# The order of two softmax steps in batches 0 and 1, and who copies the last sums

## The chip, the cores and the metric

The kernel runs on one core of a Trainium2 chip. The metric is the device time of one execution in microseconds (us); before the change it is 493.74 us, the median of three runs (493.57 to 494.34). Four engines matter here: TensorE (PE, with its weight loads as PEld), VectorE (DVE), ScalarE (ACT), and the queue of SyncE (SP), which issues most transfers.

## The reference

Two parts run one behind the other. The first is an attention between 512 tokens `x` and 32 states of each of 8 heads in 8 batches, in both directions; the second takes its result, as 4352 rows of 512 numbers, through a bilinear layer and two products.

```python
scores = scale * np.matmul(x, state.transpose(0, 1, 3, 2))
a = softmax(scores)          # over the 32 states
xread = np.matmul(a, state)
scores2 = scale * np.matmul(state, x.transpose(0, 1, 3, 2))
a2 = softmax(scores2)        # over the 512 tokens
sread = np.matmul(a2, x)
...
h = (x @ w1) * (x @ w2) @ w3
out = h @ w_out
```

(`softmax` stands for the three lines of the reference that subtract the maximum, take the exponential and divide by the sum plus 1e-9.)

## The kernel before, in words

**Precision.** Each large product is made of float32 values split in two, a high part that ACT casts (L98) and a low part that DVE takes as the difference (L99). PE then multiplies low by high, high by high and high by low.

**The stages.** At first w3 and w_out are multiplied together (L559 and L572), once for all batches, while DVE and ACT convert the float64 weights (L119 to L135) that arrive by transfers. Then come the batches. For each one, the states times w1 and w2 give `sw` (L148, split at L98 and L99), and the softmax over the states gives `at`. Their product is *stage 1* (L311): eight blocks of 128 hidden features, each with a w1 half and a w2 half in one PSUM tile `ps`. ACT copies the first half (L292), DVE multiplies it with the second (L293), and the product is split into `g_hi` and `g_lo`. *Stage 2* multiplies these with the combined weights (L325 in `project`) and stores the result. Batch 0 goes this plain way: behind each pair of blocks, `early_stage2` already does stage 2 of that pair for two of the four token tiles. Batches 1 to 7 do stage 2 in quarters (`quarter_batch`), with fewer products.

**The softmax of a batch** is a generator, `scores` in `attention_steps`, that is advanced in pieces between other work. PE makes one PSUM tile of scores (L148), in which a row is a state and a column a token. Both softmaxes start from it. For the one over the tokens, DVE takes the *token maxima* of each row (L188) and scales them (L189), and ACT takes the exponentials with them (L197) into `e`. For the one over the states, DVE *turns* the scores in 32 by 32 blocks into the tile `work` (L191), takes the maxima over the states there (L204), subtracts them (L205), and ACT takes the exponential (L208); sums, reciprocals and a multiplication follow (L213 to L216), and a second turn (L221) gives what is split into `at`. Last, DVE turns `e` into `blocks` (L228), and 16 transfers on SP (`move_blocks`, L172) lay the blocks of 32 out anew, for PE's `read_state` (L243).

**Buffers.** The tiles named `work` have two buffers. For batch 1, the turn of L191 writes into the buffer that batch 0's 16 transfers of `move_blocks` read, so it waits for all of them. The PSUM tiles of two banks have three buffers.

**What sets the order.** On PE and SP the instructions stand as the code issues them. On DVE and ACT a scheduler orders them by when it reckons that they can start and by priority, except in the opening, up to `order.close()` (L631), where they too stand as written; batch 0's softmax lies there up to the split of `at`. Batch 1's softmax is issued in `side_steps`: its first three pieces stand between blocks 4 and 5 of batch 0, right behind stage 2 of blocks 2 and 3. `PLAIN` is 1.

**The last sums.** `state_rows` handles the 256 rows of `sread` at the very end. Its two calls of `stage2` store to four places each, so `store` takes its second branch (L341 and L342): ACT copies the left half of the sums out of PSUM, DVE the right half, and then four transfers of 64 KB go out, two from ACT's queue and two from SP's (L344).

Of the kernel before, what the change touches and what calls it, by code (L numbers as in the profile page):

```python
# [27 lines left out]
ALU = mybir.AluOpType  # L28
AX = mybir.AxisListType
# [7 lines left out]
PLAIN = 1  # L37

@with_exitstack
def attn_bilinear_kernel(  # L40
# [10 lines left out]
    nc = tc.nc  # L51
# [5 lines left out]
    FT, DO = w34_k.shape[0], out.shape[2]  # L57
# [4 lines left out]
    SCALE = 1.0 / math.sqrt(D)  # L62
# [26 lines left out]
    def bank():  # L89
        return ps_o.tile([P, NF], F32, name="ps_o")  # L90

    def two_banks():
        return ps_2.tile([P, 2, NF], F32, name="ps_2")

    def split(hi, lo, src):

        return (
            nc.scalar.copy(out=hi, in_=src),  # L98
            nc.vector.tensor_tensor(out=lo, in0=src, in1=hi.bitcast(F32), op=ALU.subtract),  # L99
        )  # L100
# [41 lines left out]
    def per_head(ps, b, moving):  # L142


        for j in range(NP):
            for q in range(KT):
                rows = slice(q * D, (q + 1) * D)
                nc.tensor.matmul(  # L148
                    ps[j * NS:(j + 1) * NS, q], sts[b][rows, j], moving(rows, j), start=True, stop=True
                )  # L150
# [14 lines left out]
    def work_tile():  # L165
        return att.tile([P, KT, S], F32, name="work")
# [9 lines left out]
    def attention_steps(b):  # L176
        xd = x_tiles[b]
        a2 = {}

        def scores():  # L180

            ps = two_banks()
            per_head(ps, b, lambda rows, j: xd[rows, j])
            yield
            flat = lambda t: t.rearrange("p k s -> p (k s)")

            m2 = att.tile([P, KT], F32, name="m2")
            nc.vector.tensor_reduce(out=m2, in_=ps, axis=AX.X, op=ALU.max)  # L188
            nc.vector.tensor_scalar_mul(m2, m2, -SCALE)  # L189
            s1 = work_tile()  # L190
            nc.vector.transpose(out=flat(s1), in_=flat(ps))  # L191
            e2 = att.tile([P, KT, S], F32, name="e2", bufs=1)
            sum2 = att.tile([P, KT], F32, name="sum2")
            a2["e"], a2["sum"] = e2, sum2
            for kt in range(KT):
                one = slice(kt, kt + 1)
                nc.scalar.activation(  # L197
                    out=e2[:, kt], in_=ps[:, kt], func=AF.Exp, bias=m2[:, one], scale=SCALE, accum_out=sum2[:, one]
                )

            J = KT * S // NS
            s1v = flat(s1).rearrange("p (j n) -> p j n", n=NS)
            m1 = att.tile([P, J], F32, name="m1")
            nc.vector.tensor_reduce(out=m1, in_=s1v, axis=AX.X, op=ALU.max)  # L204
            nc.vector.tensor_tensor(  # L205
                out=s1v, in0=s1v, in1=m1.unsqueeze(2).broadcast_to([P, J, NS]), op=ALU.subtract
            )
            nc.scalar.activation(out=s1, in_=s1, func=AF.Exp, scale=SCALE)  # L208
            yield
            nc.vector.tensor_scalar_add(sum2, sum2, 1e-9)  # L210
            nc.vector.reciprocal(out=sum2, in_=sum2)
            sum1 = att.tile([P, J], F32, name="sum1")
            nc.vector.tensor_reduce(out=sum1, in_=s1v, axis=AX.X, op=ALU.add)  # L213
            nc.vector.tensor_scalar_add(sum1, sum1, 1e-9)
            nc.vector.reciprocal(out=sum1, in_=sum1)
            nc.vector.tensor_tensor(  # L216
                out=s1v, in0=s1v, in1=sum1.unsqueeze(2).broadcast_to([P, J, NS]), op=ALU.mult
            )
            yield
            at = work_tile()  # L220
            nc.vector.transpose(out=flat(at), in_=flat(s1))  # L221
            at_tiles[b] = [att.tile([P, KT, S], F32R, name=f"at_{part}", bufs=1) for part in ("hi", "lo")]
            last = split(*at_tiles[b], at)
            yield

            blocks = work_tile()
            with tc.issue_after(last[1].ins):
                nc.vector.transpose(out=flat(blocks), in_=flat(e2))  # L228
            a2["t"] = work_tile() if b < PLAIN else att.tile([P, KT, S], F32, name="e2", bufs=1)
            tiles = lambda t: t.rearrange("p k (t m) -> p (k t) m", m=P)  # L230
            move_blocks(lambda its, j: tiles(a2["t"])[its, :, j * NS:(j + 1) * NS],
                        lambda mine, c: tiles(blocks)[mine, :, c * NS:(c + 1) * NS])

        def read_state():

            xs = token_tiles[b]

            ps = (bank() if b else two_banks()[:, 0])[:, :KT * D].rearrange("p (k d) -> p k d", k=KT)
            for kt in range(KT):
                for t in range(NT):  # L240
                    for j in range(NP):
                        mine = slice(j * NS, (j + 1) * NS)
                        nc.tensor.matmul(  # L243
                            ps[mine, kt], a2["t"][:, kt, t * P + j * NS:t * P + (j + 1) * NS],
                            xs[:, t, 2 * j + kt], start=(t == 0), stop=(t == NT - 1),
                        )
            scaled = att.tile([P, KT, D], F32, name="scaled", bufs=1)
            a2["read"] = nc.vector.tensor_tensor(
                out=scaled, in0=ps, in1=a2["sum"].unsqueeze(2).broadcast_to([P, KT, D]), op=ALU.mult
            )  # L250
            turned = att.tile([P, KT, D], F32, name="turned")
            nc.vector.transpose(
                out=turned.rearrange("p k d -> p (k d)"), in_=scaled.rearrange("p k d -> p (k d)")
            )
            yield
            move_blocks(lambda its, j: sread[its, j, b * NS:(b + 1) * NS],
                        lambda mine, c: turned.rearrange("p k (c n) -> p (k c) n", n=NS)[mine, c])

        return scores, read_state, a2


# [25 lines left out]
    last_split, stored = [], []  # L287
# [47 lines left out]
    def store(ps, dests):  # L335
        o = main.tile([P, NF], F32, name="tmp", bufs=4)[:, :DO]
        with tc.high_priority():
            if len(dests) == 1:
                stored[:] = [nc.scalar.copy(out=o, in_=ps[:, :DO])]
            else:  # L340
                nc.scalar.copy(out=o[:, :DO // 2], in_=ps[:, :DO // 2])  # L341
                nc.vector.tensor_copy(out=o[:, DO // 2:], in_=ps[:, DO // 2:DO])  # L342
        for (dest, first, n), queue in zip(dests, cycle((nc.scalar, nc.sync))):
            queue.dma_start(out=dest, in_=o[first:first + n])  # L344

# [308 lines left out]
    for tt in range(NT):  # L654
        dests = [(out[0, tt * P:(tt + 1) * P], 0, P)]
# [85 lines left out]
```

## Time and profile before

| | |
|---|---|
| median of three runs | 493.74 us |
| the profiled execution, its own time | 493.72 us |
| its span, first to last instruction | 491.9 us |
| granted clock of TensorE in the span | 1.0 |
| turn (L191), 8 times | 1.23 us each |
| token maxima (L188), 8 times | 1.19 us each |

Rows of the timeline give the start in us from the span's start, the length, the engine, the line, the operation and its tiles (out<-in), their shape and how many instructions are merged; a bracket at the end is the idle time of the engine in front of it, and what ended that. Rows with SPq or ACTq are issues of transfers. A row of the chain of waits has start, length, engine, tile and line. Most of the lines stand for many instructions, so the start tells which one is meant.

### The profile page before, as it was taken

What the parts mean: (1) busy time and instruction counts of PE and PEld (TensorE: products, weight loads), DVE (VectorE), ACT (ScalarE), POOL (GpSimd) and SP (SyncE); (2) the same over time, 40 slices, a digit from 0 to 9 for tenths busy, and PEclk for the clock granted to TensorE, in tenths of its full rate; (3) what the DMA queues carried; (4) which work ended last, traced back from release to release, by engine and by line L of the source; (5) the groups of instructions that cost most, each with busy time, mean ns of one, the idle gap of its engine ahead of it and who ended that gap; (6) DMA issues with size and microseconds to landing.
All of it is one profiled execution on the core that took longest, in us unless ns stands there. A gap on an engine that the chain in (4) does not pass through costs nothing.

```text
span 491.9 us, 8604 instructions
## 1 busy us (share of the span) xinstructions
PE 483.7 (98%) x3390; PEld 368.3 (75%) x3390; DVE 391.4 (80%) x578; ACT 238.2 (48%) x364; POOL 0.2 (0%) x4
## 2 busy tenths in 40 slices
PE   7999999999999999999999999999999999999996
PEld 5444467667787878787878788877887788899885
DVE  5759897779799879957995899589859985578870
ACT  4867784443367144704570456055605550354640
POOL 0000000000000000000000000000000000000000
PEclk9999999999999999999999999999999999999999
DMA  8994971143104414130413042204220222001101
GB/s 342 414 418 135 373 294 28 16 186 86 42 7 177 105 29 179 19 102 15 179 37 94 5 180 49 81 5 179 50 79 6 89 54 75 7 2 43 45 2 43
DMA packets 56361, 52.49 MB, mean 107 GB/s; under 512 B 42752, under 2 KB 50944, under 8 KB 51712
## 3 DMA queue, kind: packets, MB, share of 16 engines
q1 hardware_dynamic: 47488, 43.27, 26.3%
q10 hardware_dynamic: 8832, 8.65, 5.1%
q8 instruction: 27, 0.44, 0.4%
q14 instruction: 14, 0.11, 0.1%
HBM read 38.27 MB, written 8.91 MB: 96 GB/s over the span
## 4 chain that ended last, share of the span: by engine, by line
PE 78%; DVE 7%; SPq 6%; ACT 5%; DMA 3%; issue 1%; ACTq 0%; DVEq 0%
PE ps L311 29%; PE ps_o L429 11%; PE ps L441 8%; SPq L172 6%; PE ps L148 6%; PE ps_o L434 5%; PE ps L446 4%; PE ps L679 3%; PE ps_o L559 3%; PE ps L559 3%; PE ps_o L325 2%; PE ps L681 2%; ACT ulps L127 2%; DMA raw<-in_w_dram 1%; ACT w_sb L119 1%; PE ps_o L243 1%
## 5 line engine op out<-in xcount | busy, mean ns | idle before, releaser
L311 PE MATMUL ps<-at_lo,sw_hi 128*128 128x512 f32 x256 | 101.8, 397 | 0.2 <-ACT e L197 0.2
L311 PE MATMUL ps<-at_hi,sw_hi 128*128 128x512 f32 x256 | 99.9, 390 | 0.0
L311 PE MATMUL ps<-at_hi,sw_lo 128*128 128x512 f32 x256 | 99.7, 389 | 0.0
L518 ACT COPY tmp<-ps 128x512 f32<-128x512 f32 x56 | 32.8, 585 | 126.0 <-PE ps L311 115.3
L311 PEld LDWEIGHTS ps<-at_lo,sw_hi 128*128 128x128 f32 x256 | 48.1, 188 | 17.6 <-DVE g_x L398 4.4
L311 PEld LDWEIGHTS ps<-at_hi,sw_lo 128*128 128x128 f32 x256 | 48.1, 188 | 10.3
L311 PEld LDWEIGHTS ps<-at_hi,sw_hi 128*128 128x128 f32 x256 | 48.1, 188 | 9.5 <-issue 0.2
L457 DVE TENSOR_TENSOR tmp<-tmp,ps 128x512 f32<-128x512 f32 x42 | 28.9, 688 | 17.3 <-PE ps L446 16.3
L398 DVE TENSOR_TENSOR g_x<-tmp,ps 128x512 f32<-128x512 f32 x28 | 19.1, 681 | 28.7 <-ACT tmp L518 28.7
L99 DVE TENSOR_TENSOR sw_lo<-ps,sw_hi 128x1024 fp32r<-128x1024 f32 (+1 forms) x34 | 38.2, 1145 | 0.2 <-ACT sw_hi L98 0.2
L98 ACT CAST g_hi<-raw 128x512 fp32r<-128x512 f32 x42 | 24.1, 618 | 23.2 <-DVE raw L398 14.3
L98 ACT CAST sw_hi<-ps 128x1024 fp32r<-128x1024 f32 (+1 forms) x34 | 31.1, 964 | 2.9 <-PE ps L148 2.7
L429 PEld LDWEIGHTS ps_o<-wo,g_hi 128*128 128x128 f32 x224 | 28.2, 191 | 5.6 <-issue 5.0
L99 DVE TENSOR_TENSOR g_lo<-raw,g_hi 128x512 fp32r<-128x512 f32 x42 | 28.0, 681 | 4.9 <-PE ps_o L434 2.8
L429 PEld LDWEIGHTS ps_o<-t,g_hi 128*128 128x128 f32 x224 | 27.8, 192 | 5.0 <-issue 5.0
L98 ACT CAST g_hi<-g_x 128x512 fp32r<-128x512 f32 x42 | 25.9, 620 | 11.5 <-DVE g_x L398 6.0
L148 PE MATMUL ps<-w_sb,st 64*32 64x512 f32 (+1 forms) x544 | 31.4, 570 | 0.0
L429 PE MATMUL ps_o<-t,g_hi 128*128 128x256 f32 x224 | 29.8, 286 | 0.0
L429 PE MATMUL ps_o<-wo,g_hi 128*128 128x256 f32 x224 | 29.7, 286 | 0.0
L99 DVE TENSOR_TENSOR g_lo<-g_x,g_hi 128x512 fp32r<-128x512 f32 x42 | 27.4, 679 | 1.8 <-PE ps_o L434 1.8
L572 PE MATMUL ps_o<-w_sb,w 128*128 128x512 f32 x64 | 28.5, 599 | 0.2 <-DVE w L135 0.2
L441 PE MATMUL ps<-t,g_hi 128*128 128x512 f32 x112 | 28.0, 392 | 0.0
(105 smaller groups left out, 784.4 us busy)
## 6 DMA issues: line engine op xcount, KB each, us to landing
raw<-in_w_k_dram SPq DMA_DIRECT2D x8, 1024.0 KB, 5.9
x_d<-in_x_d_dram SPq DMA_DIRECT2D x8, 1024.0 KB, 6.6
raw<-in_w_dram SPq DMA_DIRECT2D x8, 1024.0 KB, 6.4
x_s<-in_x_s_dram SPq DMA_DIRECT2D x8, 1024.0 KB, 5.0
out_dram<-tmp ACTq DMA_DIRECT2D x56, 128.0 KB, 1.8
raw<-in_w3t_dram SPq DMA_DIRECT2D x4, 1024.0 KB, 5.1
e<-work SPq DMA_DIRECT2D x112, 32.0 KB, 2.0
sread<-turned SPq DMA_DIRECT2D x128, 4.0 KB, 1.7
```

Of the source, the lines that this page charges most:

```text
L98: nc.scalar.copy(out=hi, in_=src),
L99: nc.vector.tensor_tensor(out=lo, in0=src, in1=hi.bitcast(F32), op=ALU.subtract),
L148: nc.tensor.matmul(ps[j * NS:(j + 1) * NS, q], sts[b][rows, j], moving(rows, j), start=True, stop=True)
L172: nc.sync.dma_start(out=dest(slice(c * NS, (c + 1) * NS), j), in_=src(slice(j * NS, (j + 1) * NS), c))
L311: nc.tensor.matmul(ps[:, i], w[:, kt, c:c + P], a[:, kt], start=(k == 0), stop=(k == 3 * KT - 1))
L429: nc.tensor.matmul(ps[:, tt * HO:(tt + 1) * HO], g, w(part, k), start=(fresh and k == 0 and tt == 0 and part == "lo"), stop=False, skip_gr ...
L434: nc.tensor.matmul(ps[:, tt * HO:(tt + 1) * HO], g, w("hi", k), start=False, stop=(k == QF - 1), skip_group_check=True)
L441: nc.tensor.matmul(ps[:, tt].rearrange("p (n d) -> p n d", n=2), g, w(k), start=(k == 0), stop=False, skip_group_check=True,)
L457: sum2 = lambda out, x, y: nc.vector.tensor_tensor(out=out, in0=x, in1=y, op=ALU.add)
L518: nc.scalar.copy(out=a_sb, in_=ps[:, 0])
L559: nc.tensor.matmul(w34_ps[i][:, :DO], chunks[k][:, DO + i * P:DO + (i + 1) * P], w_out[k], start=(k == 0), stop=(k == FT - 1),)
L572: nc.tensor.matmul(w34_ps[i][:, :DO], w3s[i][:, k * P:(k + 1) * P], w_out[k], start=(k == 0), stop=(k == FT - 1))
```

## The change

In `scores`, the buffer for the turned scores is taken ahead of the one for the maxima, and the two groups of steps, the turn on one side and the token maxima with their scaling on the other, become two small functions. Batches 0 and 1 call the turn first, batches 2 to 7 the maxima first, as all of them did before. In `store` the branch with two engines goes, and ACT copies the whole width of the sums in all cases.

```diff
+            s1 = work_tile()
             m2 = att.tile([P, KT], F32, name="m2")
-            nc.vector.tensor_reduce(out=m2, in_=ps, axis=AX.X, op=ALU.max)
-            nc.vector.tensor_scalar_mul(m2, m2, -SCALE)
-            s1 = work_tile()
-            nc.vector.transpose(out=flat(s1), in_=flat(ps))
+
+            def turn():
+                nc.vector.transpose(out=flat(s1), in_=flat(ps))
+
+            def maxima():
+                nc.vector.tensor_reduce(out=m2, in_=ps, axis=AX.X, op=ALU.max)
+                nc.vector.tensor_scalar_mul(m2, m2, -SCALE)
+
+            for step in (maxima, turn) if b > PLAIN else (turn, maxima):
+                step()
...
-            if len(dests) == 1:
-                stored[:] = [nc.scalar.copy(out=o, in_=ps[:, :DO])]
-            else:
-                nc.scalar.copy(out=o[:, :DO // 2], in_=ps[:, :DO // 2])
-                nc.vector.tensor_copy(out=o[:, DO // 2:], in_=ps[:, DO // 2:DO])
+            stored[:] = [nc.scalar.copy(out=o, in_=ps[:, :DO])]
```

The lines behind the first edit stand 7 lower in the changed kernel, those behind the second 3 lower: the exponentials of L197 are L204 there, L204 is L211, L205 is L212, L293 is L300, L213 is L220; the turn is L191 in both, the maxima are L194 and their scaling L195.

In the order of DVE, batch 0 has the five steps in the old order, and then in the new one (`ps_226` are the scores, `work` the turned scores, the `m` tiles the maxima):

```order
L188 TENSOR_REDUCE m_256<-ps_226 128x2
L189 TENSOR_SCALAR m_256<-m_256 128x2
L191 STREAM_TRANSPOSE work<-ps_226 128x1024
L204 TENSOR_REDUCE m_265<-work 128x32
L205 TENSOR_TENSOR work<-work,m_265 128x1024
```
```order
L191 STREAM_TRANSPOSE work<-ps_226 128x1024
L194 TENSOR_REDUCE m_257<-ps_226 128x2
L195 TENSOR_SCALAR m_257<-m_257 128x2
L211 TENSOR_REDUCE m_265<-work 128x32
L212 TENSOR_TENSOR work<-work,m_265 128x1024
```

What stands in front and behind is the same; the scaling now stands between the maxima and the maxima over the states.

In the order of DVE, batch 1, from the first step behind block 4 of batch 0 on. `ps_609` are batch 1's scores, `ps_638` and `ps_658` blocks 5 and 6 of batch 0 as PE leaves them; the `g_lo` in these rows is block 5's low part. Before, and then now:

```order
L188 TENSOR_REDUCE m_618<-ps_609 128x2
L191 STREAM_TRANSPOSE work<-ps_609 128x1024
L189 TENSOR_SCALAR m_618<-m_618 128x2
L204 TENSOR_REDUCE m_627<-work 128x32
L205 TENSOR_TENSOR work<-work,m_627 128x1024
L293 TENSOR_TENSOR tmp<-tmp,ps_638 128x512
L210 TENSOR_SCALAR sum_624<-sum_624 128x2
L211 RECIPROCAL sum_624<-sum_624 128x2
L213 TENSOR_REDUCE sum_633<-work 128x32
L293 TENSOR_TENSOR tmp<-tmp,ps_658 128x512
L99 TENSOR_TENSOR g_lo<-tmp,g_hi 128x512
L214 TENSOR_SCALAR sum_633<-sum_633 128x32
```
```order
L191 STREAM_TRANSPOSE work<-ps_609 128x1024
L194 TENSOR_REDUCE m_619<-ps_609 128x2
L211 TENSOR_REDUCE m_627<-work 128x32
L300 TENSOR_TENSOR tmp<-tmp,ps_638 128x512
L195 TENSOR_SCALAR m_619<-m_619 128x2
L212 TENSOR_TENSOR work<-work,m_627 128x1024
L99 TENSOR_TENSOR g_lo<-tmp,g_hi 128x512
L300 TENSOR_TENSOR tmp<-tmp,ps_658 128x512
L217 TENSOR_SCALAR sum_624<-sum_624 128x2
L218 RECIPROCAL sum_624<-sum_624 128x2
L220 TENSOR_REDUCE sum_633<-work 128x32
L99 TENSOR_TENSOR g_x<-tmp,g_x 128x512
```

Block 5's product moved from behind the subtraction to the place ahead of it, and its low part from behind the sums (L213) to right behind the subtraction; the turn with its wait for transfers moved ahead of the maxima.

In the order of ACT at the same place, from the cast of block 4's high part on (`ps_638` and `ps_658` as above; the first `g_hi` row is block 4's, the second block 5's). Before, and then now:

```order
L98 CAST g_hi<-tmp 128x512
L197 ACTIVATE e_623,sum_624<-ps_609,m_618 128x512
L292 COPY tmp<-ps_638 128x512
L197 ACTIVATE e_623,sum_624<-ps_609,m_618 128x512
L208 ACTIVATE work<-work 128x1024
L292 COPY tmp<-ps_658 128x512
L98 CAST g_hi<-tmp 128x512
```
```order
L98 CAST g_hi<-tmp 128x512
L299 COPY tmp<-ps_638 128x512
L98 CAST g_hi<-tmp 128x512
L204 ACTIVATE e_623,sum_624<-ps_609,m_619 128x512
L299 COPY tmp<-ps_658 128x512
L204 ACTIVATE e_623,sum_624<-ps_609,m_619 128x512
L215 ACTIVATE work<-work 128x1024
```

Block 5's copy and cast now stand ahead of the exponentials; before, the cast stood behind L208.

Besides, block 7 of batch 0 takes the PSUM buffer that block 5 had, where before it took that of batch 1's scores; the first read of a state takes that one now. PE's order and SP's are the same as before.

## The prediction

> **What bounds the kernel now.** The page's table of engines comes first, then the timeline of the tensor engine (PE), its rows with an idle time in brackets.
>
> ```profile
> PE 483.7 (98%) x3390; PEld 368.3 (75%) x3390; DVE 391.4 (80%) x578; ACT 238.2 (48%) x364; POOL 0.2 (0%) x4
> ```
> ```profile
> 51.01 7.13 PE L572 MATMUL ps_o<-w_sb,w 128*128 128x512 f32 x16 [0.19 <-DVE w L135]
> ...
> 96.94 0.73 PE L325 MATMUL ps_o<-wo,g_hi 128*128 128x512 f32 x2 [0.24 <-ACT g_hi L98]
> ...
> 98.40 0.50 PE L325 MATMUL ps_o<-wo,g_lo 128*128 128x512 f32 x1 [0.73 <-DVE g_lo L99]
> ...
> 137.88 0.50 PE L311 MATMUL ps<-at_lo,sw_hi 128*128 128x512 f32 x1 [0.24 <-ACT e L197]
> ```
>
> PE is the bound, and behind its first matmul on weights these are the only four places where it waits. So a microsecond on the vector engine (DVE) or the scalar engine (ACT) is worth something only if it shortens one of the four, or lies behind PE's last matmul. The change touches three: batch 0's softmax stands ahead of 51.01, batch 1's between 89.8 and 104, the last stores behind everything. Batches 2 to 7 keep their order.
>
> What the second and third wait cost is read from PE's rows around them, and from its pace in the chain of waits.
>
> ```profile
> 95.18 0.61 PE L325 MATMUL ps_o<-wo,g_hi 128*128 128x512 f32 x2
> ...
> 99.44 0.40 PE L311 MATMUL ps<-at_lo,sw_hi 128*128 128x512 f32 x1
> ```
> ```profile
> 476.88 10.92 PE ps_o L325 x48
> ```
>
> Undisturbed, a matmul of L325 takes 10.92/48 = 0.2275 us. The twelve of this place (hidden blocks 4 and 5 of batch 0) begin at 95.18 and should be through at 97.91; the next stage begins at 99.44. So 1.53 us are lost, more than the 0.97 in the brackets, since PE is also slower around a stall: a matmul that starts behind one has 0.50 in its row (98.40), one that doesn't 0.40 (99.44), so a restart costs 0.1.
>
> **Batch 0, ahead of 51.01.** The timeline of DVE and ACT:
>
> ```profile
> 38.09 1.21 DVE L188 TENSOR_REDUCE m<-ps 128x2 f32<-128x1024 f32 x1
> ...
> 39.34 0.17 DVE L189 TENSOR_SCALAR m<-m 128x2 f32<-128x2 f32 x1
> 39.42 1.24 DVE L191 STREAM_TRANSPOSE work<-ps 128x1024 f32<-128x1024 f32 x1
> ...
> 40.69 1.22 DVE L204 TENSOR_REDUCE m<-work 128x32 f32<-128x1024 f32 x1
> 40.75 0.69 ACT L197 ACTIVATE e<-ps,m 128x512 f32<-128x512 f32 x1 [1.77 <-DVE work L191]
> ...
> 41.95 1.23 DVE L205 TENSOR_TENSOR work<-work,m 128x1024 f32<-128x1024 f32 x1
> ...
> 43.20 1.06 ACT L208 ACTIVATE work<-work 128x1024 f32<-128x1024 f32 x1 [1.01 <-DVE work L205]
> ...
> 49.73 1.23 DVE L135 CUSTOM_DVE_ANT_0 w<-w,ulps 128x2048 uint16<-128x2048 uint16 x1
> ```
>
> From 38.09 to the conversion at 49.73, for which PE waits at 51.01, DVE stands in no row idle: it is a chain, and what it saves PE saves. The five steps stay; what changes is which of them must wait for the one in front. Spacings, start to start: a step that waits for a 1024-wide one begins 1.25 to 1.26 after it (38.09 to 39.34, 40.69 to 41.95), one that doesn't wait sooner:
>
> ```profile
> 112.34 1.23 DVE L228 STREAM_TRANSPOSE work<-e 128x1024 f32<-128x1024 f32 x1
> 113.50 1.18 DVE L99 TENSOR_TENSOR t<-raw,t 128x1024 fp32r<-128x1024 f32 x1
> ```
> ```profile
> 179.45 1.18 DVE L188 TENSOR_REDUCE m<-ps 128x2 f32<-128x1024 f32 x1
> 180.56 1.22 DVE L191 STREAM_TRANSPOSE work<-ps 128x1024 f32<-128x1024 f32 x1
> ```
>
> Turn to maxima 1.16, maxima to their scaling 1.25, scaling to L204 0.08, L204 to L205 1.26: 3.75, where 38.09 to 41.95 is 3.86. DVE gains 0.11. ACT's exponentials of L197 start at 40.75 behind the turn; now they follow the scaling, at 38.09+1.16+1.25+0.17 = 40.67: no loss, and ACT idles 1.01 before L208 anyway. PE's wait at 51.01 falls by 0.11. Bounds: 0 to 0.19, the bracket.
>
> **Batch 1, where most of it lies.** DVE's order is not only exchanged: the scheduler places the next steps anew. The chain of waits and the timeline of DVE and ACT:
>
> ```profile
> 89.08 1.93 DMA work<-work
> ...
> 91.03 1.25 DVE work L191
> ```
> ```profile
> 89.77 1.22 DVE L188 TENSOR_REDUCE m<-ps 128x2 f32<-128x1024 f32 x1 [1.06 <-PE ps L148]
> ...
> 92.43 0.69 ACT L197 ACTIVATE e<-ps,m 128x512 f32<-128x512 f32 x1 [4.45 <-DVE m L189]
> ...
> 93.11 0.58 ACT L292 COPY tmp<-ps 128x512 f32<-128x512 f32 x1
> ...
> 94.15 0.21 ACT L197 ACTIVATION_READ_ACCUMULATOR e<-ps,m 128x1 f32 x1
> ...
> 94.72 0.68 DVE L293 TENSOR_TENSOR tmp<-tmp,ps 128x512 f32<-128x512 f32 x1
> ...
> 95.31 0.16 DVE L210 TENSOR_SCALAR sum<-sum 128x2 f32<-128x2 f32 x1
> ...
> 96.26 0.62 ACT L98 CAST g_hi<-tmp 128x512 fp32r<-128x512 f32 x1
> ...
> 97.66 0.68 DVE L99 TENSOR_TENSOR g_lo<-tmp,g_hi 128x512 fp32r<-128x512 f32 x1
> ...
> 99.41 1.22 DVE L216 TENSOR_TENSOR work<-work,sum 128x1024 f32<-128x1024 f32 x1
> ```
>
> The turn writes the buffer that batch 0's last 16 transfers read, so it waits for the one that lands at 91.01. Before, the maxima fill that wait (89.77 to 90.99); now DVE stands idle until 91.03 with everything queued behind the turn, and the maxima follow: 1.16 us more of DVE work behind the landing. But block 5's product (L293) now comes ahead of the scaling and the subtraction, and its low part right behind the subtraction. From 91.03, with the spacings above (1.16 behind a turn, 1.11 behind a reduction): maxima 92.19, L204 93.30, L293 94.41 (its copy, 0.58 long at 93.11, stands ahead of the exponentials now and is done in time). Scaling +0.59 (as 94.72 to 95.31) 95.00, subtraction +0.08 95.08, low part +1.15 (the same wide step as a turn) 96.23, done 96.91. The high part on ACT (0.62 at 96.26) follows L293's end at 95.09 and is done at 95.74. PE wants them for its 7th and 9th matmul, at 95.18 + 6 × 0.2275 = 96.54 and 97.00, their weights a step sooner: the first wait goes, of the second about one restart, 0.1, remains. PE gains 1.53 − 0.1 = 1.42, if the transfers land as before. Without the new places of L293 and the low part, the 1.16 would fall on PE instead.
>
> What is late next? The softmax of batch 1 itself. ACT now does block 5's cast first (until 95.74), then the two exponentials with a copy between them (92.43 to 94.36 before, so 1.93) until 97.67, then L208 (1.06) until 98.73. On DVE the reduction L213 follows, and 1.11 later a low part. From a low part to L216 it took 1.75 (97.66 to 99.41), with a second low part of 0.6 in between that now stands elsewhere: L216 begins near 98.75 + 1.11 + 1.15 = 101.0, 1.6 later than before, and block 7's L293 1.15 behind it, near 102.2. But:
>
> ```profile
> 103.07 0.69 DVE L293 TENSOR_TENSOR tmp<-tmp,ps 128x512 f32<-128x512 f32 x1 [2.43 <-ACT tmp L292]
> ...
> 126.91 1.30 PE L243 MATMUL ps_o<-x_s,e 128*32 128x64 f32 x64
> ```
> ```profile
> 124.80 0.70 SPq L172 DMA_DIRECT2D e<-work x1
> ...
> DMA to landing us min/median/max: 1.9/2.0/4.2
> ```
>
> DVE idled 2.43 there for PE, which covers the 1.6. Without that cover they would hold up all that follows. With it L293, and what DVE does behind it up to the turn of the blocks at 112.34 and the 16 transfers that wait for that, comes 0.87 earlier. Three places then take from PE's 1.42. The matmuls of the next weights (L148) want block 7's bank from L293, which is 0.87 earlier, PE 1.42: they may wait 0 to 0.55; PE showed no bracket there, so I take 0.2, and 1.2 is left. At 126.91 PE needs the last of the 16 transfers, issued at 124.80 and by the median landed at 126.80: it lands near 125.93 now, PE comes at 125.7, and 0.95 is left. At 137.88 PE waits for ACT's exponentials of batch 2. That chain starts at PE's blocks 0 and 1, ahead of the read, and keeps the 1.2. PE comes at 137.88 − 0.24 − 0.1 − 0.95 = 136.6, the exponentials end 1.2 earlier, at 136.7: that wait shrinks, and batch 1 is worth 1.2 in all (bounds 0.6 and 1.5: the read gains nothing, or none of the three waits appears). Behind it PE waits nowhere, so the gain stays.
>
> **The last sums.** The timeline of ACT and DVE at the end, and a whole copy by ACT alone:
>
> ```profile
> 487.83 0.37 ACT L341 COPY tmp<-ps_o 128x256 f32<-128x256 f32 x1 [5.01 <-PE ps_o L325]
> 488.23 0.42 DVE L342 COPY tmp<-ps_o 128x256 f32<-128x256 f32 x1 [4.96 <-ACT tmp L341]
> 488.69 0.85 ACTq L344 DMA_DIRECT2D out_dram<-tmp x2
> ```
> ```profile
> 107.62 0.59 ACT L339 COPY tmp<-ps_o 128x512 f32<-128x512 f32 x1 [1.18 <-PE ps_o L325]
> 108.24 0.39 ACTq L344 DMA_DIRECT2D out_dram<-tmp x1
> ```
>
> The halves run one after the other: DVE's waits for ACT's. Transfers start 0.86 after the copy's start (487.83 to 488.69); alone it is 0.62 (107.62 to 108.24). Gain 0.24, all at the end. The same edit on the store at 482.44 is hidden under PE's matmuls until 487.8.
>
> The Trainium skill, TensorEngine Tiling (Array Packing), section PSUM Bottleneck, says to use both ScalarE and VectorE to empty PSUM, which speaks against this edit; by it two halves side by side would cost the longer one, 0.42, the edit would lose 0.17, and the sum would be 0.41 higher. The trace disagrees, since L342's row names L341 as what it waited for.
>
> **The sum.** 0.11 + 1.2 + 0.24 = 1.55. The profiled execution took 493.72 us (span 491.9, 1.8 around it); the median of the three runs is 493.74, so they can stand for each other. 493.72 − 1.55 = 492.17, say 492.2. A measurement of this kernel tells about 0.2%, 1.0 us, from no change.
>
> **The rivals.**
> - *Given back at the read* (0.13). The exponentials or L216 take longer than the spacings say, the 16 transfers don't come earlier, and PE waits at 126.91 for nearly all that it won. Against it stands the 0.87 of margin on L293. Then batch 1 gives the 0.11 between landing (126.80) and use and most of the 0.34 plus the slow start at 137.88, some 0.6 in all: 493.72 − 0.11 − 0.6 − 0.24 = 492.8, at the edge of what can be told.
> - *The transfers land late* (0.12 with no difference that can be told, 0.05 slower). The turn heads DVE's queue now, and by as much as batch 0's transfers land later, the low part of block 5 comes later, and PE. For it: the slowest of batch 1's transfers took 4.2 from issue to landing, the median 2.0. One us late leaves 1.42 − 1.0 of PE's gain: 493.72 − 0.11 − 0.42 − 0.24 = 492.95. From 1.7 late on it is slower than before: then L293 of block 7 comes 0.83 after its old time, and so do the 16 transfers, the read loses 0.83 less the slack of 0.11, the wait at 137.88 gives 0.34 back, and 0.38 is as much as the two ends win. At 3 late it is 493.72 + 3 − 0.87 − 0.11 − 0.34 − 0.35 = 495.05. Against: nothing ahead of those transfers changes but the 0.11, which makes them earlier.
> - *Halves side by side at the end* (0.05). If the split copy costs the longer half alone, 0.42, the whole one loses 0.17 where I count 0.24 won: 492.2 + 0.41 = 492.6. The bracket at 488.23 speaks against it. This is the case in which the Trainium skill's rule of TensorEngine Tiling (Array Packing), section PSUM Bottleneck, would hold here.
>
> My forecast has 0.65, its own range 491.8 to 492.6. Faster: 0.65, the 0.05 and a sixth of the first rival, 0.72; same: the rest of that and the 0.12, 0.23; slower 0.05. The range goes from 491.7 (no new wait in batch 1: 1.5) to 493.1, which leaves out the latest landings.
>
> **What would show it.** Right: the turn first at 91 with idle DVE ahead of it; block 5's low part done near 96.9; no bracket at L325's high part and one under 0.2 at its low part; the stage at 99.44 beginning near 97.9 (with the 0.11 of batch 0); last transfers issued 0.62 behind the copy's start. Wrong: a bracket of over 0.5 at L243 near 126, a turn that starts later than 91.2, or a wait in batches 2 to 7 that was not there.

## The result, and the profile after

The changed kernel took 491.78 us (median of 6 runs, 491.68 to 491.93) against 494.16 for the kernel before in the 6 runs beside it (493.57 to 496.23): a ratio of 0.9948, with a 95% interval of 0.993 to 0.9965. That is faster, and below the forecast of 492.2 and its ratio of 492.2/493.74 = 0.9969. As a time 491.78 lies at the low end of the stated range of 491.7 to 493.1; as a gain, 2.38 is more than the 2.04 to which the range goes from 493.74. Measured again (the experiment *changed again*, below) it was 492.13 against 493.56, 0.9971 with 0.9959 to 0.9983, a gain of 1.43. Both kernels differ between the two measurements. The kernel before scatters upwards: over the 102 executions of this study it has a median of 493.67, 21 of them above 494 and two above 496, and four of those 21 are among the six of the first measurement. The changed kernel has a median of 491.83 over 12 executions, 491.68 to 491.93 in the first measurement and 491.71 to 492.49 in the second. So the gain is about 1.8 by the medians over all executions; the two profiled executions, 493.72 and 491.68, differ by 2.04. The forecast counted 1.55.

The table of engines and, under it, the chain of waits by engine, of the changed kernel:

```profile
PE 483.7 (99%) x3390; PEld 369.0 (75%) x3390; DVE 390.3 (80%) x576; ACT 238.6 (49%) x364; POOL 0.2 (0%) x4
...
PE 92%; DVE 3%; ACT 2%; DMA 1%; issue 0%; ACTq 0%; DVEq 0%
```

PE does the same work in the same 483.7 us; its share rises because the span is 2.0 shorter, 489.9. So the gain is idle time of PE that went, and 0.24 behind its last matmul. PE's timeline at the places that the prediction names:

```profile
95.01 0.61 PE L332 MATMUL ps_o<-wo,g_hi 128*128 128x512 f32 x2
...
96.37 0.61 PE L332 MATMUL ps_o<-wo,g_hi 128*128 128x512 f32 x2
96.82 0.39 PE L332 MATMUL ps_o<-wo,g_lo 128*128 128x512 f32 x1
...
97.73 0.39 PE L318 MATMUL ps<-at_lo,sw_hi 128*128 128x512 f32 x1
...
101.57 1.95 PE L148 MATMUL ps<-w_sb,st 64*32 64x512 f32 x32
...
125.17 1.10 PE L250 MATMUL ps_o<-x_s,e 128*32 128x64 f32 x64
...
136.15 0.50 PE L318 MATMUL ps<-at_lo,sw_hi 128*128 128x512 f32 x1 [0.20 <-ACT e L204]
```

Of the four brackets one is left. Comparing starts with those of before tells where the time came from: 95.18 to 95.01 is batch 0's 0.17; 99.44 to 97.73 is 1.71, so batch 1 gave the whole 1.53 of its two waits; 126.91 to 125.17 (1.74) and 137.88 to 136.15 (1.73) show that nothing of it was given back. The twelve matmuls run through without a restart, 97.73 − 95.01 = 2.72 = 12 × 0.227.

Batch 0's five steps on DVE:

```profile
38.07 1.24 DVE L191 STREAM_TRANSPOSE work<-ps 128x1024 f32<-128x1024 f32 x1
39.23 1.18 DVE L194 TENSOR_REDUCE m<-ps 128x2 f32<-128x1024 f32 x1
40.45 0.17 DVE L195 TENSOR_SCALAR m<-m 128x2 f32<-128x2 f32 x1
40.53 1.21 DVE L211 TENSOR_REDUCE m<-work 128x32 f32<-128x1024 f32 x1
41.77 1.22 DVE L212 TENSOR_TENSOR work<-work,m 128x1024 f32<-128x1024 f32 x1
```

38.07 to 41.77 is 3.70, forecast 3.75, before 3.86. In batch 1, the timeline of DVE with one row of ACT (the cast of block 5's high part):

```profile
90.34 1.25 DVE L191 STREAM_TRANSPOSE work<-ps 128x1024 f32<-128x1024 f32 x1 [1.82 <-DMA work<-work]
91.52 1.18 DVE L194 TENSOR_REDUCE m<-ps 128x2 f32<-128x1024 f32 x1
...
93.75 0.67 DVE L300 TENSOR_TENSOR tmp<-tmp,ps 128x512 f32<-128x512 f32 x1
...
94.41 1.22 DVE L212 TENSOR_TENSOR work<-work,m 128x1024 f32<-128x1024 f32 x1
95.54 0.68 DVE L99 TENSOR_TENSOR g_lo<-tmp,g_hi 128x512 fp32r<-128x512 f32 x1
...
100.22 1.23 DVE L223 TENSOR_TENSOR work<-work,sum 128x1024 f32<-128x1024 f32 x1
101.36 0.68 DVE L300 TENSOR_TENSOR tmp<-tmp,ps 128x512 f32<-128x512 f32 x1
```
```profile
94.45 0.62 ACT L98 CAST g_hi<-tmp 128x512 fp32r<-128x512 f32 x1 [1.32 <-DVE tmp L300]
```

The turn waits for the transfers with DVE idle, as forecast, but it starts at 90.34 and not at 91.03. Why it does is taken up at the end. Measured from its start all is as forecast: block 5's low part +5.20 (forecast 96.23 − 91.03 = 5.20), block 7's product at 101.36 +11.02 (forecast 11.17). Block 5's parts are ready at 95.07 and 96.22, PE takes them at 96.37 and 96.82. At the end, ACT's copy and its two transfers:

```profile
486.03 0.59 ACT L345 COPY tmp<-ps_o 128x512 f32<-128x512 f32 x1 [4.80 <-PE ps_o L332]
486.65 0.85 ACTq L347 DMA_DIRECT2D out_dram<-tmp  x2
```

The copy starts 1.80 earlier than before, the transfers 2.04: the edit itself gives 0.24.

### The profile page after: what moved, and what is told of

Same layout as the page of the kernel before. It is cut to its first block, busy times and chain, and to the rows that moved or that the text cites. A ratio compares the mean times of both kernels' runs of the same rounds, so it can differ in the third digit from the quotient of the medians.

```text
span 489.9 us, 8603 instructions
## 1 busy us (share of the span) xinstructions
PE 483.7 (99%) x3390; PEld 369.0 (75%) x3390; DVE 390.3 (80%) x576; ACT 238.6 (49%) x364; POOL 0.2 (0%) x4
## 4 chain that ended last, share of the span: by engine, by line
PE 92%; DVE 3%; ACT 2%; DMA 1%; issue 0%; ACTq 0%; DVEq 0%
PE ps L318 34%; PE ps_o L432 11%; PE ps L444 8%; PE ps L148 7%; PE ps_o L332 7%; PE ps_o L437 5%; PE ps L449 4%; PE ps L682 3%; PE ps_o L575 3%; PE ps_o L562 3%; PE ps L562 3%; PE ps L684 2%; PE ps_o L250 1%; DMA raw<-in_w_k_dram 1%; DVE m L194 0%; ACT ulps L127 0%
## 5 line engine op out<-in xcount | busy, mean ns | idle before, releaser
L148 PE MATMUL ps<-w_sb,st 64*32 64x512 f32 (+1 forms) x544 | 31.4, 570 | 0.0
```

The lines of the kernel that those rows point to most:

```text
L148: nc.tensor.matmul(ps[j * NS:(j + 1) * NS, q], sts[b][rows, j], moving(rows, j), start=True, stop=True)
```

## The experiments

The theory after this result: three gains that add up, 0.17 for batch 0, some 1.55 for batch 1 and 0.24 for the last sums; batch 1's comes from the place of block 5's product and low part, which the scheduler chose anew, and not from the exchange itself. The rivals: batch 1's gain comes from the turn starting earlier; or it hangs on an early landing of the transfers in the executions measured.

**Each part alone.** The kernel before with the new order in batch 0 only, in batch 1 only, and with the last sums only. The first two are shown as edits of the changed kernel's line; their store is that of the kernel before, and the third has the changed store alone.

```diff
-            for step in (maxima, turn) if b > PLAIN else (turn, maxima):
+            for step in (turn, maxima) if b == 0 else (maxima, turn):    # first kernel
+            for step in (turn, maxima) if b == 1 else (maxima, turn):    # second kernel
```

> Only batch 0 turns the scores first; batch 1 and the last sums as before. Theory (three separate gains): PE's wait near 51 goes, PE is 0.17 us earlier from there on, and the waits near 97 and 98.4 stay as long as before (0.24 and 0.73), so 0.1 to 0.3 us less than before. Rival (batch 0's exchange also makes batch 0's transfers land much earlier and so takes batch 1's waits away): 1 us or more less.

> Only batch 1 turns the scores first; batch 0 and the last sums as before. Theory: PE's two waits near 97 and 98.4 go and 1.3 to 1.6 us are won; the turn starts when the last of batch 0's transfers lands, near 91.0, and the low part of block 5 ends near 96.9. Rival (the gain needs the transfers 0.7 us earlier, as the profile of the changed kernel has them): 0.8 us or less, with a wait of half a microsecond at the low part or at the read near 126.

> Only the last sums are copied by ACT alone. Theory: the last transfers are issued 0.62 us behind the copy's start instead of 0.86, and the span is 0.24 us shorter; nothing else moves. Rival (two engines copy faster than one): 0.17 us longer.

Batch 0 alone: 493.49, ratio 0.9995 (0.9986 to 1.0004); batch 1 alone: 492.47, 0.9976 (0.9966 to 0.9987); last sums alone: 493.46, 0.9998 (0.9989 to 1.0007). The first and the last are too small to show in the time of a whole run, so the profiles have to carry them. PE with batch 0 alone, and then with batch 1 alone:

```profile
98.14 0.50 PE L332 MATMUL ps_o<-wo,g_lo 128*128 128x512 f32 x1 [0.73 <-DVE g_lo L99]
```
```profile
50.95 7.13 PE L579 MATMUL ps_o<-w_sb,w 128*128 128x512 f32 x16 [0.20 <-DVE w L135]
...
136.29 0.50 PE L318 MATMUL ps<-at_lo,sw_hi 128*128 128x512 f32 x1 [0.23 <-ACT e L204]
```

Each kernel loses the waits of its own part and keeps the others: with batch 0 alone the one at 51 is gone and the one at 98 stays, with batch 1 alone it is the other way round. With the last sums alone the copy starts at 487.81 and the transfers 0.62 later, in place of 0.86. The spans are 491.7, 490.3 and 491.7 where the kernel before has 491.9: 0.2 + 1.6 + 0.2 = 2.0, the whole change, so in the profiles the parts don't touch each other. The medians say less: against 493.67 the three give 0.18, 1.20 and 0.21, 1.59 in all. The executions with batch 1 alone go from 492.12 to 493.16, and the profiled one is of the fastest. Its turn starts at 90.24; what the slower ones lose was not profiled.

**Where batch 1's gain comes from.** Two kernels part the exchange from what it set off. In the first, all is as before, but block 5's product, cast and low part are ordered ahead of the rest of batch 1's softmax (whose first two pieces are issued apart for that, with the order of SP's and PE's work kept); in the second, the changed kernel's product and low part are held back to the places that they had before.

```diff
+            with tc.issue_after(product5[0].ins) if b == 1 else ExitStack():    # first kernel
                 nc.vector.tensor_tensor(
                     out=s1v, in0=s1v, in1=m1.unsqueeze(2).broadcast_to([P, J, NS]), op=ALU.subtract
                 )
+            with tc.issue_after(last_split[0].ins) if b == 1 else ExitStack():
                 nc.scalar.activation(out=s1, in_=s1, func=AF.Exp, scale=SCALE)
...
+            with after(0):    # second kernel: behind the subtraction of batch 1
                 nc.vector.tensor_tensor(out=a_sb[:, :n], in0=a_sb[:, :n], in1=ps[:, 1, :n], op=ALU.mult)
+            with after(1):    # behind its sums
                 last_split[:] = split(g_hi, g_lo, a_sb[:, :n])
```

> Batch 1 takes the maxima first, as before, and so do batch 0 and the last sums; only block 5's product, cast and low part are placed where the changed kernel has them: the product ahead of the subtraction, the low part right behind it, the cast ahead of the exponential over the states. Theory (the gain of batch 1 is the place of block 5's parts, and the exchange of turn and maxima only brought it about): PE's waits near 97 and 98.4 go and 1.3 to 1.7 us are won, as much as with the exchange or a little more. Rival (the gain comes from the turn standing first): 0.3 us or less.

> The changed kernel with all three edits, but on DVE block 5's product is held behind batch 1's subtraction and its low part behind the sum over the states, where they stood before; the turn stays first. Theory (the gain is the place of block 5's parts): PE waits at block 5's low part for 1 to 2 us, longer than before the change, since the maxima now lie behind the landing; the time is 1.8 to 2.8 us above the changed kernel, so about that of before or up to 0.8 above. Rival (the turn standing first is worth something by itself): at least 1 us below before.

With the parts ahead: 492.12, ratio 0.9967 (0.9955 to 0.998), span 490.4, though its maxima come first and its turn starts later than in the profile of before (91.74 for 91.03). DVE and PE there:

```profile
91.74 1.25 DVE L191 STREAM_TRANSPOSE work<-ps 128x1024 f32<-128x1024 f32 x1 [0.70 <-DMA work<-work]
...
96.17 0.69 DVE L99 TENSOR_TENSOR g_lo<-tmp,g_hi 128x512 fp32r<-128x512 f32 x1
```
```profile
97.73 0.39 PE L328 MATMUL ps_o<-wo,g_lo 128*128 128x512 f32 x1
97.96 0.39 PE L314 MATMUL ps<-at_lo,sw_hi 128*128 128x512 f32 x1
```

So 1.5 of the gain needs no exchange: the place of block 5's parts is shown to be the cause. Nor does it need an early landing here: the turn waits for transfers that land at 91.72, the latest of the twelve profiles without added transfers, but the maxima lie ahead of it and not behind. With the parts behind: 495.89 (493.83 to 496.3), ratio 1.0032 (1.0019 to 1.0045), 4 us above the changed kernel and, which the expectation did not have, 2 above the kernel before. Its PE:

```profile
97.88 0.73 PE L336 MATMUL ps_o<-wo,g_hi 128*128 128x512 f32 x2 [1.39 <-ACT g_hi L98]
99.33 0.80 PE L336 MATMUL ps_o<-wo,g_lo 128*128 128x512 f32 x1 [0.72 <-DVE g_lo L99]
```

The waits are 1.14 longer in all than before, since the maxima now stand between the turn and them. The rest is a thing that shows in the granted clock, in windows of 1 us (window, PE's busy time, clock, share of DMA, GB/s):

```profile
96.00:97.00 1.00, 0.49 (x3) 1.00 0.00 0
97.00:98.00 1.00, 0.12 (x1) 1.00 0.00 0
98.00:99.00 1.00, 0.61 (x2) 1.00 0.00 0
99.00:100.00 1.00, 0.67 (x2) 0.61 0.00 0
100.00:101.00 1.00, 1.00 (x4) 0.50 0.00 0
101.00:102.00 1.00, 1.00 (x3) 0.50 0.00 0
102.00:103.00 1.00, 1.00 (x4) 0.68 0.00 0
103.00:104.00 1.00, 1.00 (x6) 1.00 0.00 0
```

PE runs at half its clock for 3.4 us behind the waits (0.78 + 1 + 1 + 0.64 of these windows), and a matmul takes 0.63 for 0.39. Half of 3.4 is an estimate of what it costs, 1.7. Of the ten executions, the six with a mean clock of 0.997 or less took 495.79 to 496.3, the four others 493.83 to 494.33: the medians are 1.8 apart.

**The later batches too.** All eight batches turn first.

```diff
-            for step in (maxima, turn) if b > PLAIN else (turn, maxima):
+            for step in (turn, maxima):
```

> The changed kernel, but all batches turn the scores first. Theory: in batch 2 the token maxima's scaling falls behind other work on DVE, the exponentials come 1 to 2 us later, and PE's wait near 136 (0.20 in the changed kernel) grows by about as much; in batches 3 to 7 PE has room; 1 to 2 us above the changed kernel, so 0 to 1 us below before. Rival (turning first is good everywhere): at or below the changed kernel.

492.77, ratio 0.9979 (0.997 to 0.9989): 1.0 above the changed kernel, but not at 136, where the bracket is 0.24. The turns of L191 follow each other after 48.38 there and 48.21 in the changed kernel, from batch 3 on. ACT and PE in the stage of batch 5:

```profile
278.84 0.69 ACT L204 ACTIVATE e<-ps,m 128x512 f32<-128x512 f32 x1 [2.09 <-DVE m L195]
```
```profile
278.18 0.39 PE L318 MATMUL ps<-at_hi,sw_hi 128*128 128x512 f32 x1
278.40 0.39 PE L318 MATMUL ps<-at_hi,sw_lo 128*128 128x512 f32 x1
278.78 0.50 PE L318 MATMUL ps<-at_lo,sw_hi 128*128 128x512 f32 x1
```

ACT's exponentials stand in front of the copies that free PE's banks, and they wait for the scaled maxima. Counted from the first of the two steps, the scaling (L195) starts 3.96 later here (274.69 to 278.65) and 2.26 later in the changed kernel (274.13 to 276.39). PE's step from 278.40 to 278.78 is 0.38 for 0.23; a batch is 0.17 longer, and six of them make the 1.0. In these batches the maxima first is right: the turn has no bracket in the changed kernel, so it waits for no transfer that they could fill.

**A later landing.** Two transfers of 4 KB from `blocks` into a spare tile go ahead of batch 0's 16, in the kernel before and in the changed one.

```diff
+            if b == 0:
+                spare = att.tile([P, 32], F32, name="spare", bufs=1)
+                for q in range(2):
+                    rows = slice(q * 32, (q + 1) * 32)
+                    nc.sync.dma_start(out=spare[rows], in_=flat(blocks)[rows, :32])
```

> The kernel before with two more small transfers (4 KB each, into a tile that nobody reads) ahead of batch 0's 16, so that these are issued and land about 1.3 us later. Theory (the landing sets the turn and PE's wait behind it): 1.0 to 1.4 us above before. Rival (the landing is not what PE waits for): within 0.3 us of before.

> The changed kernel with the same two more small transfers ahead of batch 0's 16. Theory (with block 5's parts ahead the low part has a few tenths of a microsecond of room against the landing, and behind that is held by it): PE waits again at block 5's low part, by 0.5 to 1.0 us, and the time is 0.6 to 1.2 us above the changed kernel, so 0.8 to 1.5 us below before. Rival (no room): 1.3 us above it. Rival (PE no longer depends on the landing): as the changed kernel.

498.12, ratio 1.0089 (1.0072 to 1.0106), and 495.87, 1.005 (1.0033 to 1.0067). Both are some 4 us longer, and most of that has nothing to do with the landing: the turns follow each other after 48.57 in both. The matmuls of L311 are slower, in the groups by line (with shapes; here its lines are L316), first this kernel, then the one with a wider spare tile:

```profile
L316 PE MATMUL ps<-at_hi,sw_lo 128*128 128x512 f32 x256 | 101.1, 395 | 0.0
```
```profile
L316 PE MATMUL ps<-at_hi,sw_lo 128*128 128x512 f32 x256 | 99.7, 389 | 0.0
```

So this pair told nothing of the landing. Three kernels followed: a spacer alone, and both again with a spare tile of 256 bytes per partition.

```diff
-    const.tile([P, 32], F32, name="pad_1")
+    const.tile([P, 64], F32, name="pad_1")    # the spacer alone
...
-                spare = att.tile([P, 32], F32, name="spare", bufs=1)
+                spare = att.tile([P, 64], F32, name="spare", bufs=1)    # the two others
```

> The kernel before, with nothing but a spacer in SBUF made 128 bytes per partition longer (256 for 128), so that every tile behind it lies 128 bytes further on; no instruction is added or moved. In the two runs with added transfers the batches followed each other after 48.57 us in place of 48.21, and the hidden layer's matmuls of the later batches started 0.232 apart in place of 0.227; they too had one more tile of 128 bytes. Theory (the addresses of the tiles did that, not the transfers): the batches are 48.5 to 48.6 apart here too, 7 x 0.36 = 2.5 us more in all, 496.2; the waits near 97 to 99 us are those of the kernel before. Rival (the transfers did it): nothing moves, 493.7.

> The kernel before, with the two added 4 KB transfers of the earlier run, their tile 256 bytes per partition in place of 128 (only the first 128 are written). A spacer of 128 bytes by itself left the batches 48.2 apart, so the addresses alone are no sure cause of the slower matmuls. Theory (it is still where this tile puts the tiles behind it, and 256 bytes put them back in step; the later landing is paid in full in the kernel before): batches 48.2 apart, the first turn of batch 1 some 0.8 later than in the profile of before, 494.4 to 495.0. Rival one (the chain from the landing has slack in the kernel before as well): 493.7 to 494.0. Rival two (the transfers, or any such tile, slow the matmuls): batches 48.5 or more apart, 497 to 498.

> The changed kernel, with the same two transfers and the tile of 256 bytes. Theory (in the changed kernel block 5's low part is 0.7 to 1.4 us ahead of what TensorE needs, so a landing 1.2 us later costs near nothing at 97 us; what it costs lies in the read of batch 1, at the next wait near 136): 491.8 to 492.8, so the gap to the kernel before with the same transfers is as large as without them or larger, 2.0 to 3.0. Rival one (batch 1's gain hangs on an early landing): the gap shrinks to 1.2 or less. Rival two (the transfers, or any such tile, slow the matmuls): 495 to 496.

The spacer alone: 494.14, ratio 1.001 (1.0001 to 1.0019), batches 48.2 apart. So a shift of all that lies behind the constants by 128 bytes is not the cause. It costs 0.4, which neither expectation had; in its profile PE is 0.29 later at the wait near 138 (138.17 for 137.88) and 0.37 at its last matmuls, and why stays open. With 256 bytes the batches are 48.2 apart again, with the same instructions and transfers: it is the size of that tile in its pool. Which tiles then lie badly to each other stays open.

Now the landing can be read. The kernel before with the transfers, PE:

```profile
97.52 0.73 PE L330 MATMUL ps_o<-wo,g_hi 128*128 128x512 f32 x2 [0.83 <-ACT g_hi L98]
98.98 0.50 PE L330 MATMUL ps_o<-wo,g_lo 128*128 128x512 f32 x1 [0.72 <-DVE g_lo L99]
```

Its turn starts at 91.62, 0.59 later than in the kernel before, and the waits grow by 0.58: paid in full. In time it is 496.26, ratio 1.0042 (1.0025 to 1.0059), since in seven of the 12 executions the mean clock is 0.997 or less again (496.08 to 497.88); the five others took 494.15 to 494.89, about what the theory has. The profiled execution is one of the five, so that the clock fell at this place in the seven is argued from the kernel with the parts behind, and not shown. The changed kernel with the transfers, DVE and then PE:

```profile
92.47 1.25 DVE L191 STREAM_TRANSPOSE work<-ps 128x1024 f32<-128x1024 f32 x1 [3.65 <-DMA work<-work]
```
```profile
97.25 0.73 PE L337 MATMUL ps_o<-wo,g_hi 128*128 128x512 f32 x2 [0.43 <-ACT g_hi L98]
98.40 0.50 PE L337 MATMUL ps_o<-wo,g_lo 128*128 128x512 f32 x1 [0.42 <-DVE g_lo L99]
```

It took 493.34 (492.69 to 494.31), ratio 0.9987 (0.9977 to 0.9998), more than the theory's 492.8. This execution landed 2.13 later than the changed kernel's, and PE's next stage begins at 99.44 in place of 97.73, of which 0.28 was lost ahead of it. So 1.43 is paid at 97, and the slack is 2.13 − 0.28 − 1.43 = 0.4, not the 0.7 to 1.4 of the theory. The gap between the two kernels is 2.9 by the medians and 494.59 − 493.34 = 1.25 without the executions of lowered clock: the rival with the early landing has a part in it. The two profiles don't compare like with like, though: the transfers landed at 91.44 in the one and at 92.19 in the other.

**All parts without the exchange in batch 1.** Batch 0 and the last sums as changed, batch 1 with its maxima first and block 5's parts ahead (the edit shown above).

> Batch 0 as the changed kernel has it (turn first), batch 1 with its maxima first as before but block 5's product, cast and low part ahead of the scores' exponentials, last sums by ScalarE alone. Theory (all that batch 1 gains comes from the place of block 5's parts, and the exchange of turn and maxima gives nothing there by itself): the sum of the parts, -0.2 for batch 0, -1.5 for the parts ahead, -0.2 for the last sums, 491.8 as the changed kernel. Rival (the turn first in batch 1 is worth something by itself, since the chain to batch 1's weights starts 1.2 us earlier): 492.2 to 492.6.

491.83, ratio 0.9964 (0.995 to 0.9977): the changed kernel's time, and no kernel of this study beats it. The transfers landed at 91.33 in its profile, 1.06 later than in the changed kernel's, and PE has no bracket near 97. Two of the five executions took 492.33 and 492.4. The profiled one is the first of these, and PE loses time early in it, where the other kernels' profiles have no bracket:

```profile
75.98 1.95 PE L148 MATMUL ps<-w_sb,st 64*32 64x512 f32 x32 [0.44 <-DVE tmp L303]
```

**Changed again, and the two halves.** The changed kernel once more, and a version that copies the last sums by two engines into two tiles:

```diff
+        right = main.tile([P, NF], F32, name="tmp", bufs=4)[:, :DO // 2]
+        left = o[:, :DO // 2]
...
+            nc.scalar.copy(out=left, in_=ps[:, :DO // 2])
+            nc.vector.tensor_copy(out=right, in_=ps[:, DO // 2:DO])
...
+            queue.dma_start(out=dest[:, :DO // 2], in_=left[first:first + n])
+            queue.dma_start(out=dest[:, DO // 2:], in_=right[first:first + n])
```

> The changed kernel once more, beside many runs of the kernel before on the same chip. Theory (the gain is the sum of the three parts, 2.0, and the first measurement's 494.16 for the kernel before came from a few runs with a late landing or a lowered clock): 491.7 to 491.9 against 493.7. Rival (the gain is 2.4 or more): 491.3 or less against 493.7. By the forecast's sum of 1.55 it would be 492.15.

> The changed kernel, but the last sums are again copied half by ScalarE and half by VectorE, and now into two separate tiles in SBUF, each with its own transfers (eight of 32 KB at the end for four of 64 KB). Theory (the halves stand one behind the other because they read one bank of PSUM): VectorE's copy still starts about 0.4 behind ScalarE's, its row names ScalarE as what it waited for, and the time is that of the changed kernel plus 0.2 to 1.2 (more transfers are issued, 0.6 each). Rival (the shared tile made them wait): both start together, and the first transfers go out 0.4 to 0.5 behind the copy's start in place of 0.62.

Changed again: 492.13 (491.71 to 492.49), ratio 0.9971 (0.9959 to 0.9983); two of the six are in the theory's 491.7 to 491.9, the median is not, and it is next to the 492.15 of the forecast's sum. Its profiled execution has the span of 490.0 and the turn at 90.29. What the executions above 492 lose was not profiled. Two tiles: 492.25, ratio 0.9974 (0.9965 to 0.9984), 0.1 above the changed kernel beside it. Its DVE at the end (ACT's half starts at 486.67):

```profile
487.07 0.42 DVE L354 COPY tmp<-ps_o 128x256 f32<-128x256 f32 x1 [4.96 <-ACT tmp L353]
```

The halves still run one behind the other, 0.40 from copy to copy, though they share no tile in SBUF any more, so the rival is out. What they share is the PSUM tile that both read, one bank. The row names ACT's copy as what DVE waited for: DVE waits for a semaphore that this copy raises at its end, so the wait stands in the program. The Trainium skill, PSUM — Partial Sum Buffer, section PSUM bank collisions raise a hardware error, says that two engines must be kept off one bank and quadrant of it, reads too. This row agrees, with DVE held for 0.40 by a copy of 0.37 that, too, only reads the bank. Halves from two banks were not tried, so that the bank is the reason is argued and not shown.

## Why the prediction was right and wrong

- *What bounds the kernel.* Right: the gain is idle time of PE and the tail, and nothing else moved.
- *Batch 0*: 0.17 for 0.11. The chain on DVE was 0.05 shorter still than the spacings said. The upper bound of 0.19 held.
- *Batch 1, the cause.* Right, and shown from both sides: block 5's parts in the new place give the gain without the exchange, and with the exchange but the old places it is a loss. The prediction put 1.16 on PE for that case; the waits grew by 1.14, and the lowered clock came on top.
- *Batch 1, the size*: 1.2 was forecast, and the profiles give about 1.6 (PE's last matmuls start at 484.48 for 486.27, 1.79, less batch 0's 0.17). This is the step that failed: PE's gain was counted "if the transfers land as before", with the turn waiting "for the one that lands at 91.01". That landing was one execution's, and the transfers landed 0.74 earlier in the profiled execution of the changed kernel. A landing comes behind 16 issues on SP, of which one takes longer than the others' 0.61 (min/median/max in ns, before and now):

```profile
L172 SPq DMA_DIRECT2D work<-work x16: 600/609/1716, 78.1 to 89.1; - x16
L172 SPq DMA_DIRECT2D work<-work x16: 600/609/1292, 77.7 to 88.3; - x16
```

The long one took 0.99 to 1.95 in the twelve profiles without added transfers, and the last landing was between 90.16 and 91.72. In the old order the maxima hide an early landing. In the profile of before the two ended at once, the maxima at 90.99 and the transfers at 91.01; with the last sums alone the transfers had landed at 90.63, and the turn still starts at 91.03, right behind the maxima:

```profile
89.89 1.23 DVE L188 TENSOR_REDUCE m<-ps 128x2 f32<-128x1024 f32 x1 [1.07 <-PE ps L148]
91.03 1.24 DVE L191 STREAM_TRANSPOSE work<-ps 128x1024 f32<-128x1024 f32 x1
```

In the new order the turn starts at the landing, whenever that is: at 90.34, 90.29 and, with batch 1 alone, 90.24. Of the 0.69 by which 90.34 is earlier than 91.03, batch 0 gave 0.17 and the shorter issue 0.43. The long issue has a median of 1.17 over the twelve profiles, so the 1.72 under the forecast was a long one. The prediction priced a later landing as a rival, and an earlier one not at all beyond batch 0's 0.11. With the 0.69 the restart of 0.1 goes, and block 7's product comes 1.71 earlier and not 0.87, so that the three places which "then take from PE's 1.42" take nothing: L148 at 101.57 takes its usual time, the read at 125.17 has no bracket, the one at 136.15 is 0.20 and moved with the rest. Two of the three do show where the transfers land late: in the changed kernel with the added ones L148 takes 2.03 and the read has a bracket of 0.29. The upper bound for batch 1, 1.5 where "none of the three waits appears", was the case that came, and 0.1 more. By the medians batch 1 alone gave 1.20, as forecast; how much of the rest every execution has is open.
- *The last sums*: 0.24, as forecast. Halves side by side are out: in the kernel before and with two tiles the second waits for the first.
- *The level.* The sum was taken from 493.72, and the kernel before has a median of 493.67: right. The first measurement put it at 494.16 by a run of 496.23 and three above 494. So of the 0.83 by which its gain of 2.38 is over the forecast's 1.55, 0.44 is the level and 0.39 the changed kernel's own time (491.78 for 492.17). That the kernel before can take up to 2.5 more in an execution was no term of the sum; that a late landing or a lowered clock does it is likely from the experiments, but none of those executions was profiled.
- *The rivals.* Given back at the read: no. Late transfers: their price was right (a turn at 92.47 leaves PE at 99.44, where the kernel before had it), but without more transfers in front no profile had them land later than 91.72.

## What to carry to other kernels

Where two waits end within hundredths of a microsecond of each other, the one that the profile names is only the later one of that execution: ask what the step would wait for if either went, and look at the other executions. When an edit lets a scheduler place instructions anew, the edit and the new places are two changes; price them apart, and fix the place by hand if that is what pays. And give a wait of TensorE more than its own length: where waits of 1.5 to 2.1 us in all stood close together, the mean clock was lowered in 13 of 22 executions here, and these took 1.8 to 2.5 longer than the others.

## What the runs showed of the hardware

- TensorE's granted clock fell to 0.50 for 3.4 us behind two waits of 1.39 and 0.72 in which it was busy for 1.2 of 3 us (96 to 99). With waits of 2.1 in all in the profiled execution the mean clock was 0.997 or less in 6 of 10 executions, with 1.55 in 7 of 12, with 0.85 in none of 12, and among the 102 of the kernel before (0.97) two took over 496. The Trainium skill, TensorE: Matmul & The Clock Gate, section Part 1: The HAM clock gate (the "warmup" mystery), has half the clock after an idle window of about 3.4 us. The half agrees with this trace; no single wait was longer than 1.39, so an idle time of that length was not needed here.
- The same matmuls took 395 or 389 ns, and a batch 48.57 or 48.20 us, by whether an unrelated tile in SBUF had 128 or 256 bytes per partition; a spacer of 128 bytes further ahead did not do it.
- SyncE's issues of the 16 transfers take about 0.61 each, but in each profile one of them took 0.99 to 1.95, and the last transfer landed 1.92 to 1.93 behind the start of its issue in all but one of the twelve profiles without added ones.
- Two halves of one PSUM bank, copied by two engines, follow each other after 0.40 even with separate destinations. The wait stands in the program, as a semaphore; what the chip would do without it is not shown.
